# Attention and GELU layers on one core: opening with four-bank exponentials and split numerators, two output tiles in turns, the last one in column halves

## The chip, the core and the metric

The kernel runs on one core of a Trainium2 chip. A core has five engines that run side by side: TensorE (PE, matrix products; its weight loads are listed apart as PEld), VectorE (DVE), ScalarE (ACT), GpSimd (POOL) and SyncE (SP, which here only issues transfers). Each takes its own instructions in the order of the program and waits on semaphores for the others. PE writes its results to PSUM, which has 8 banks of 512 fp32 columns on 128 partitions. The other data lies in SBUF. Transfers are issued by SP or by POOL and run on 16 DMA engines.

The metric is the device time of one execution in microseconds. The kernel before takes 344.38 us (median of three runs, 344.34 to 344.93).

## The reference

```
# q, k, v: (8, 8, 576, 64) fp32; f: (8, 8, 576); w_in: (512, 2048); w_out: (2048, 512)
scores = q @ k^T / 8
cum    = cumsum(log(clip(f, 1e-4, 1)))
scores = where(j > i, -1e9, scores + cum[i] - cum[j])
attn   = softmax(scores) @ v                      # per batch and head
x      = attn, heads side by side                 # (4608, 512)
out    = gelu_tanh(x @ w_in) @ w_out              # (4608, 512) fp32
```

The factor exp(cum[i]) cancels in the softmax. So the kernel takes exponentials of the plain scores and scales the rows of v, and the weights of the denominators, by exp(-cum[j] - 64).

## The kernel before

The 64 pairs of batch and head are worked on in 16 *quads* of four heads. Quads 2b and 2b + 1 belong to batch b.

For each quad there are three **score rounds** (`score_round`). A round computes up to 512 columns of transposed scores for four heads into two PSUM tiles of two banks each. Two `ACTIVATE Exp` instructions (L190), each over one tile (128 x 1024 elements), write them to `pt` as bf16. In the opening the causal mask is added on PE by extra products with `lows` (L186). Later it is POOL that zeroes the entries of `pt` (`mask`, L202).

Three **products** per quad follow (`product`, L218): denominators (weights `w_bf`), and the numerators for the even and the odd half of the head dimension (weights `vw`, which `make_vw` builds out of `v_nat` and `wT` at L140). `reciprocals` turns the denominators into `rb` by a transpose, a reciprocal and a transpose on DVE (L240 to L244). `normalise` multiplies a numerator in PSUM by `rb` into `xT` on DVE (L249).

For each batch `mlp_in` multiplies `xT` by `w_in_sb` in 16 blocks `ft` of 128 hidden features (L263, 8 matmuls of 288 columns each), and ACT applies the GELU (L272) into `gT`. `mlp_out` is a generator: each step is one `ft` of one output tile of 128 tokens (one matmul of 512 columns, or four on 32 rows each). After the 16th step of a tile DVE copies the PSUM tile to SBUF (L300) and SP sends it out (L301). Its PSUM pool has two tiles of one bank. The steps are pulled between the score rounds of coming quads, in numbers written out by hand: for batch 0, 3 and then 14, 8 and 8 in the rounds of quad 2, 5, 6 and 5 in those of quad 3, 4, 4 and 3 in those of quad 4. So the 33rd step is the last of quad 2's third round.

PSUM before: tag `s` two tiles of two banks, `po` one tile of two banks, and the last two banks are `x` (one tile) in the opening and `m` (two tiles of one bank) afterwards.

The **opening** (`startup`) loads f, q, k and v, forms `cum` and `wT`, transposes k and q of quads 0 and 1, and runs six score rounds and six products. Warm-up matmuls on a blank tile keep PE busy at the start and between the rounds (L319, 11, then 6, then 4 after each of the first four rounds). Its loads on POOL's queue, in order: k and q of quads 0 and 1, v (heads 4 to 7 of batch 0), w_in in four transfers of 512 KB, k and q of quad 2, w_out in four transfers, k and q of quad 3, and v of batch 1 (heads 0 to 3, five transfers). SP issues v of batch 1 (heads 4 to 7) once q of quad 3 has landed. POOL's issues wait so that no more than eight of its transfers are under way. The order of instructions on each engine is that of the code (`manual_schedule`).

In `step(i, j, ...)`, which runs the three rounds of quad i with the products of quad j, quads 2 and 3 have `make_vw` on DVE in the third round, ahead of that round's pull of output steps. Later quads have it on POOL in the first.

Of the kernel before, what the change touches and what calls it, by code (L numbers as in the profile page):

```python
# [8 lines left out]
FP32 = mybir.dt.float32  # L9
BF16 = mybir.dt.bfloat16  # L10
AF = mybir.ActivationFunctionType
# [5 lines left out]
def kernel(  # L17
# [10 lines left out]
    nc = tc.nc  # L28
# [30 lines left out]
    psS = ctx.enter_context(tc.tile_pool(name="psS", bufs=2, space=bass.MemoryType.PSUM))  # L59
    psO = ctx.enter_context(tc.tile_pool(name="psO", bufs=1, space=bass.MemoryType.PSUM))  # L60

    def many(n, shape, dtype, name):
        return [singles.tile(shape, dtype, name=f"{name}{i}") for i in range(n)]
# [14 lines left out]
    w_in_sb = many(2, [128, N_DT, D_FF // 2], BF16, "w_in_sb")  # L78
# [10 lines left out]
    pools = {"s": psS, "po": psO}  # L89


    def after(ins, other):

# [20 lines left out]
    w_out_hbm = moe_w_out.rearrange("(u p y) n -> p u y n", p=128, y=2)  # L114

    def load_w_in(c):
        n = slice(D_FF // 2 * c, D_FF // 2 * (c + 1))
        for u in range(QPB):
            nc.gpsimd.dma_start(out=w_in_sb[c][:, 2 * u:2 * u + 2, :], in_=w_in_hbm[u, :, :, n])  # L119

    def load_w_out(c):
        n = N_FT // 8
# [21 lines left out]
    def bank_pair(tag, name):  # L144
        return pools[tag].tile([128, 2, 512], FP32, name=name, tag=tag)
# [9 lines left out]
    def score_round(i, r, tags=("s", "s"), masked=False):  # L155
        off, parts = rounds[r]
        n = sum(x[2] for x in parts)
        tiles = [bank_pair(x, "ps_s") for x in tags]
        kk, qq, p = kT[i % 2], qT[i % 2], pt[i % 2]
        def block(c, m0, m, k0, q0, nq, c0, fresh):  # L160
            for h in range(4):
                nc.tensor.matmul(  # L162
                    tiles[h // 2][m0:m0 + m, h % 2, c0:c0 + nq],
                    kk[32 * h:32 * h + 32, k0:k0 + m, c],
                    qq[32 * h:32 * h + 32, q0:q0 + nq, c],
                    start=(c == 0 and fresh), stop=(c == 1),
                    skip_group_check=True,
                )
# [12 lines left out]
        if masked:  # L181
            for g in range(2):
                c0 = 0
                for (t, q0, nq) in parts:
                    for x in range(2 if q0 == 128 * t else 0):
                        nc.tensor.matmul(tiles[g][:, x, c0:c0 + 128], ident, lows[t > 0],  # L186
                                         start=False, stop=True, skip_group_check=True)
                    c0 += nq
        for g in range(2):
            nc.scalar.activation(p[:, 2 * g:2 * g + 2, off:off + n],  # L190
                                 tiles[g][:, :, 0:n], AF.Exp, scale=scale)
# [59 lines left out]
    def denominators(i):  # L251
        reciprocals(i, product(i, den_groups(i), bank_pair("po", "po")))

    def attn_out(i, y, tag="po"):
        normalise(i, y, product(i, out_groups(i, y), bank_pair(tag, "po")))

    def mlp_mm(b, ft, ph, dts):
        hS = S // 2
        n = 256 * (ft // 2) % (D_FF // 2)
        w = w_in_sb[2 * ft // N_FT][:, :, n + ft % 2:n + 256:2]  # L260
        for dt in dts:
            for j in range(2):
                nc.tensor.matmul(  # L263
                    ph[:, j, 0:hS],
                    w[:, dt],
                    xT[b % 2][:, dt, hS * j:hS * (j + 1)],
                    start=(dt == 0), stop=(dt == N_DT - 1),
                )
# [7 lines left out]
    def mlp_in(b, fts, tag="s"):  # L276
        tiles = [bank_pair(tag, "ps_h") for _ in fts]
        for dts in (range(N_DT - 1), range(N_DT - 1, N_DT)):
            for ft, ph in zip(fts, tiles):
                mlp_mm(b, ft, ph, dts)  # L280
        for ft, ph in zip(fts, tiles):
            gelu(b, ft, ph)


    out_cols = [128]

    def mlp_out(tiles):

        for n in tiles:
            ps = pools["m"].tile([128, D_MODEL], FP32, name="pso", tag="m")  # L290
            c = 128 * (n % 9)
            for ft in range(N_FT):
                w = out_cols[0]
                for m in range(0, 128, w):
                    nc.tensor.matmul(ps[m:m + w, :], gT[:, ft, c + m:c + m + w],  # L295
                                     w_out_sb[:, ft, :], start=(ft == 0),
                                     stop=(ft == N_FT - 1), skip_group_check=True)
                if ft == N_FT - 1:
                    st = ostage_pool.tile([128, D_MODEL], FP32, name="o_st", tag="o")
                    nc.vector.tensor_copy(st, ps)  # L300
# [20 lines left out]
    def startup():  # L321
# [6 lines left out]
        make_lows()  # L328

        nc.vector.memset(blank, 0.0)  # L330
        warm = bank_pair("po", "warm")
        warm_up(warm, 11)
        nc.vector.memset(ones_f32, 1.0)
        nc.vector.memset(shift, -64.0)
# [9 lines left out]
        cum = bank_pair("x", "small")[:, 0, 0:NT * BH]  # L344
# [12 lines left out]
        make_vw(1, nc.vector)  # L357
        load_w_in(0)
        load_w_in(1)
        load_qk(2)  # L360
# [6 lines left out]
        for r, tags in enumerate((("s", "s"), ("x", "s"), ("s", "x"))):  # L367
            score_round(0, r, tags, True)
            warm_up(warm, 4)
        score_round(1, 0, masked=True)  # L370
        warm_up(warm, 4)
        score_round(1, 1, ("x", "s"), True)
        denominators(0)
        score_round(1, 2, ("s", "x"), True)
        attn_out(0, 0)
        attn_out(0, 1, "s")
        pod, po0, po1 = (bank_pair(x, "po") for x in ("s", "po", "x"))
        reciprocals(1, product(1, den_groups(1), pod))
        r0 = product(1, out_groups(1, 0), po0)
        r1 = product(1, out_groups(1, 1), po1)  # L380
        ph0, ph1 = (bank_pair("s", "ps_h") for _ in range(2))
        mlp_mm(0, 0, ph0, (0, 1))
        normalise(1, 0, r0)
        normalise(1, 1, r1)
# [16 lines left out]
    def step(i, j, fill, fills):  # L401
        for r in range(3):
            if i is not None:
                score_round(i, r)
            if j is not None:
                if r == 0:
                    denominators(j)
                else:
                    attn_out(j, r - 1, "s" if i is None and r == 1 else "po")
            if (i, r) in ((2, 0), (3, 1)):  # L410
                transpose_qk(i + 1)
            if i is not None and r > 0:
                mask(i, r - 1)
            if i is not None and r == (2 if i < 4 else 0):
                make_vw(i, nc.vector if i < 4 else nc.gpsimd)
            pull(fill, fills[r], 32)
            if i is not None and r == 2:
                mask(i, 2)
                if i == 2:
                    load_v(2)  # L420
                elif i < 5:
                    load_qk(i + 2)
# [7 lines left out]
                    load_qk(i + 2)  # L430

    with tc.manual_schedule():
        with tc.tile_pool(name="psX", bufs=1, space=bass.MemoryType.PSUM) as pools["x"]:
            startup()
        pools["m"] = ctx.enter_context(
            tc.tile_pool(name="psM", bufs=2, space=bass.MemoryType.PSUM))
        fill = none
        for b in range(B):

# [7 lines left out]
                if b + 2 < B:  # L447
                    load_v(b + 2)
            for ft in range(2, N_FT):
                mlp_in(b, (ft,), "po" if b == 0 and ft == 2 else "s")  # L450
            fill = mlp_out(out_tiles(b))
            if b == 0:
                pull(fill, 3)
# [41 lines left out]
```

## Time and profile before

| | |
|---|---|
| median of 3 runs | 344.38 us (344.34 to 344.93) |
| the profiled execution | 345.22 us |
| its span, first to last instruction | 343.5 us |
| PE busy | 333.7 us (97%) |
| ACT busy | 198.8 us (58%) |
| DVE busy | 125.3 us (36%) |
| POOL busy | 113.7 us (33%) |
| granted PE clock | 1.00 |

A row of a timeline gives the start in us, the busy time, the engine, the line of the kernel, the operation, the tile written and the tiles read, their shapes and how many instructions were merged into the row. In brackets stands the idle time ahead of it and what ended that wait. A row of the groups gives, behind the bar, the busy time and the mean duration in ns of one, and behind the second bar the idle time before them. PE's instructions are pipelined, so the rows of neighbouring products overlap. A row of a window of DMA queues gives the queue, its packets, MB, and the time of its packets as a share of 16 engines (it may pass 100%). A row of issues gives the number of transfers, the KB of each and the median time from issue to landing.

### The profile page before, as it was taken

What the parts mean: (1) busy time and instruction counts of PE and PEld (TensorE: products, weight loads), DVE (VectorE), ACT (ScalarE), POOL (GpSimd) and SP (SyncE); (2) the same over time, 40 slices, a digit from 0 to 9 for tenths busy, and PEclk for the clock granted to TensorE, in tenths of its full rate; (3) what the DMA queues carried; (4) which work ended last, traced back from release to release, by engine and by line L of the source; (5) the groups of instructions that cost most, each with busy time, mean ns of one, the idle gap of its engine ahead of it and who ended that gap; (6) DMA issues with size and microseconds to landing.
All of it is one profiled execution on the core that took longest, in us unless ns stands there. A gap on an engine that the chain in (4) does not pass through costs nothing.

```text
span 343.5 us, 11040 instructions
## 1 busy us (share of the span) xinstructions
PE 333.7 (97%) x5032; PEld 198.1 (58%) x5050; DVE 125.3 (36%) x169; ACT 198.8 (58%) x244; POOL 113.7 (33%) x157
## 2 busy tenths in 40 slices
PE   7989999899999999999999999999999999999995
PEld 2457634477445764467444774457544675557642
DVE  7591167550451513541333503434233402530011
ACT  4866677766655666656746566656745566516400
POOL 6742344844262503524163132624044401200000
PEclk9999999999999999999999999999999999999999
DMA  7899998779110870139111490109111100110021
GB/s 128 177 168 211 211 193 202 149 139 225 44 65 32 171 138 32 63 78 205 28 66 57 106 204 23 48 32 213 27 47 52 62 1 2 35 63 31 2 87 66
DMA packets 45439, 33.37 MB, mean 97 GB/s; under 512 B 34288, under 2 KB 34288, under 8 KB 45392
## 3 DMA queue, kind: packets, MB, share of 16 engines
q0 software_dynamic: 7232, 14.81, 24.3%
q1 hardware_dynamic: 38160, 17.85, 19.6%
q8 instruction: 39, 0.64, 0.8%
q14 instruction: 8, 0.07, 0.1%
HBM read 36.85 MB, written 9.44 MB: 135 GB/s over the span
## 4 chain that ended last, share of the span: by engine, by line
PE 80%; DMA 11%; issue 2%; ACT 2%; POOL 2%; SPq 2%; DVE 1%; POOLq 0%; ACTq 0%
PE ps_h L263 32%; PE pso L295 32%; PE po L218 8%; PE ps_s L162 7%; DMA w_out_sb<-in_moe_w_out_dram 5%; DMA w_in_sb<-in_moe_w_in_dram 3%; DMA q_c<-in_q_dram 2%; ACT pt L190 2%; SPq L105 1%; POOL v_nat L105 1%; DMA v_nat<-in_v_dram 1%; POOL k_c L99 0%; DVE den L240 0%; DVE o_st L300 0%; POOL w_in_sb L119 0%
## 5 line engine op out<-in xcount | busy, mean ns | idle before, releaser
L295 PE MATMUL pso<-w_out_sb,gT 128*32 128x512 bf16 (+1 forms) x1892 | 131.6, 379 | 1.1 <-DMA w_out_sb<-in_moe_w_out_dram 0.4
L263 PE MATMUL ps_h<-xT,w_in_sb 128*128 128x288 bf16 x1024 | 128.3, 286 | 0.7 <-DMA w_in_sb<-in_moe_w_in_dram 0.7
L190 ACT ACTIVATE pt<-ps_s 128x1024 bf16<-128x1024 f32 x96 | 93.0, 1021 | 50.0 <-PE ps_s L162 47.6
L272 ACT ACTIVATE gT<-ps_h 128x576 bf16<-128x576 f32 x128 | 82.5, 651 | 64.7 <-PE ps_h L263 64.6
L263 PEld LDWEIGHTS <-w_in_sb 128*128 128x128 bf16 x1024 | 99.5, 98 | 30.4 <-issue 3.2
L295 PEld LDWEIGHTS <-gT 128*32 128x32 bf16 (+1 forms) x1908 | 59.0, 97 | 54.0 <-issue 1.5
L202 POOL TENSOR_SCALAR_AFFINE_SELECT pt<-pt 128x512 bf16<-128x512 bf16 (+1 forms) x70 | 45.3, 656 | 125.4 <-ACT pt L190 124.4
L300 DVE COPY o_st<-pso 128x512 f32<-128x512 f32 x36 | 24.6, 684 | 63.0 <-PE pso L295 62.8
L240 DVE STREAM_TRANSPOSE den<-po 128x576 f32<-128x576 f32 x16 | 12.5, 782 | 80.5 <-PE po L218 80.5
L249 DVE TENSOR_TENSOR xT<-po,rb 128x576 bf16<-128x576 f32 x32 | 24.1, 757 | 44.9 <-PE po L218 44.5
L162 PE MATMUL ps_s<-qT,kT 32*64 32x64 bf16 (+6 forms) x896 | 36.1, 292 | 1.4 <-DVE qT L130 0.5
L140 POOL TENSOR_TENSOR vw<-v_nat,wT 128x1280 bf16<-128x1280 f32 (+1 forms) x24 | 34.8, 1473 | 1.6 <-PE po L218 1.5
L162 PEld LDWEIGHTS <-kT 32*128 32x128 bf16 (+1 forms) x896 | 15.1, 97 | 26.9 <-issue 23.3
L218 PE MATMUL po<-pt,vw 128*32 128x64 bf16 (+4 forms) x768 | 27.3, 279 | 0.3 <-DVE den L240 0.3
L130 DVE STREAM_TRANSPOSE kT<-k_c 128x576 f32<-128x576 f32 x16 | 19.9, 1246 | 19.5 <-DMA k_c<-in_k_dram 19.5
L218 PEld LDWEIGHTS <-vw 128*32 128x32 bf16 x768 | 13.2, 97 | 14.0 <-issue 7.0
L130 DVE STREAM_TRANSPOSE qT<-q_c 128x576 f32<-128x576 f32 x16 | 19.9, 1243 | 0.8 <-DMA q_c<-in_q_dram 0.6
L99 POOL DMA_DIRECT2D k_c<-in_k_dram x16 | 9.1, 568 | 31.6 <-DVE kT L130 26.6
L218 PE MATMUL po<-pt,w_bf 128*32 128x512 bf16 (+5 forms) x384 | 14.3, 279 | 0.9 <-POOL pt L202 0.9
L244 DVE STREAM_TRANSPOSE rb<-rec 128x576 f32<-128x576 f32 x16 | 12.5, 779 | 0.5
L190 ACT ACT_TABLE_LOAD x7 | 9.0, 1283 | 5.9 <-PE ps_s L162 5.9
L99 POOL DMA_DIRECT2D q_c<-in_q_dram x16 | 8.7, 544 | 9.7 <-DVE qT L130 5.3
(38 smaller groups left out, 72.9 us busy)
## 6 DMA issues: line engine op xcount, KB each, us to landing
out_dram<-o_st SPq DMA_DIRECT2D x36, 256.0 KB, 2.0
v_nat<-in_v_dram SPq DMA_DIRECT2D x24, 256.0 KB, 7.1
k_c<-in_k_dram POOLq DMA_DIRECT2D x16, 288.0 KB, 6.3
q_c<-in_q_dram POOLq DMA_DIRECT2D x16, 288.0 KB, 7.1
w_in_sb<-in_moe_w_in_dram POOLq DMA_DIRECT2D x4, 512.0 KB, 10.9
w_out_sb<-in_moe_w_out_dram POOLq DMA_DIRECT2D x4, 512.0 KB, 18.5
v_nat<-in_v_dram SPq DMA_DIRECT2D x14, 128.0 KB, 5.8
v_nat<-in_v_dram POOLq DMA_DIRECT2D x8, 128.0 KB, 7.0
```

Source lines behind the costliest of these rows:

```text
L99: return [nc.gpsimd.dma_start(out=dst[i % 2].rearrange("p a d -> p (a d)"), in_=src[b, h0:h0 + 4].rearrange("h (p a) d -> (h p) (a d)", p=32))
L130: nc.vector.transpose(out=dst[i % 2].rearrange("p s c -> p (s c)").bitcast(FP32) .rearrange("p (t a) -> p a t", a=S // 32), in_=src[i % 2] ...
L140: eng.tensor_mul(vw[i % 2][:p, slot:slot + n], v_nat[(i // QPB) % 2][:p, 0:n, h0:h0 + 4, :], wT[:p, i, 0:n, :].unsqueeze(3).to_broadcast([ ...
L162: nc.tensor.matmul(tiles[h // 2][m0:m0 + m, h % 2, c0:c0 + nq], kk[32 * h:32 * h + 32, k0:k0 + m, c], qq[32 * h:32 * h + 32, q0:q0 + nq, c ...
L190: nc.scalar.activation(p[:, 2 * g:2 * g + 2, off:off + n], tiles[g][:, :, 0:n], AF.Exp, scale=scale)
L202: nc.gpsimd.affine_select(out=p[p0:p1, :, o:o + 128], in_=p[p0:p1, :, o:o + 128], compare_op=ALU.is_ge, fill=0.0, base=0, pattern=[[0, 4]] ...
L218: nc.tensor.matmul(po[r0:r0 + w.shape[-1], o:o + nq], w, p[:, h, col:col + nq], start=(n < 2), stop=(n in (0, len(product_parts) - 1)), sk ...
L249: nc.vector.tensor_mul(xT[i // QPB % 2][:, 2 * (i % QPB) + y, :], po, rbs[i])
L263: nc.tensor.matmul(ph[:, j, 0:hS], w[:, dt], xT[b % 2][:, dt, hS * j:hS * (j + 1)], start=(dt == 0), stop=(dt == N_DT - 1),)
L272: nc.scalar.activation(gT[:, ft, o:o + S].rearrange("p (j n) -> p j n", j=2), ph[:, :, 0:hS], AF.Gelu_apprx_tanh)
L295: nc.tensor.matmul(ps[m:m + w, :], gT[:, ft, c + m:c + m + w], w_out_sb[:, ft, :], start=(ft == 0), stop=(ft == N_FT - 1), skip_group_chec ...
L300: nc.vector.tensor_copy(st, ps)
```

## The change

1. **PSUM and exponentials in the opening.** A pool `q` of two tiles of four banks takes all eight banks while `startup` runs. A score round fills one tile, and one `ACTIVATE Exp` of 128 x 2048 elements reads all four banks. The warm-up matmuls between the rounds are gone; the 11 and the 6 ahead of them stay. All six rounds come first, and the products follow in `first_products`, in pools `s`, `po` and `x` that are opened when `q` is closed.
2. **Numerators of quad 0.** ACT copies each of the two from PSUM to SBUF (`num`), and POOL multiplies them by `rb`. Before, DVE multiplied straight out of PSUM. The loads of w_out, of k and q of quad 3 and of v of batch 1 are issued after these two POOL products.
3. **w_in in three tiles**, of 512, 512 and 1024 columns: six transfers in place of four.
4. **Output tiles 0 and 1** take turns: 12 steps of tile 0, 12 of tile 1, the last 4 of tile 0, the last 4 of tile 1. Tile 2 follows as before, with step 33.
5. **`make_vw` of quad 3** goes from DVE in the third round to POOL in the second.
6. **The last output tile** is computed in two column halves: 16 matmuls of 256 columns, a copy and a transfer for each half.
7. Block `ft` = 2 of batch 0 uses a tile of tag `s` in place of `po`.

```diff
+        if whole:
+            four = pools["q"].tile([128, 4, 512], FP32, name="ps_s", tag="q")
+            tiles = [four[:, 0:2, :], four[:, 2:4, :]]
...
+            nc.scalar.activation(p[:, :, off:off + n], four[:, :, 0:n], AF.Exp, scale=scale)
+            return
...
     def mlp_out(tiles):
+        half, open_ps = D_MODEL // 2, {}
+        most, whole = range(N_FT - 4), [(n, range(N_FT), 0, D_MODEL) for n in tiles]
+        if tiles[0] == 0:
+            whole[0:2] = [(n, fts, 0, D_MODEL) for fts in (most, range(N_FT - 4, N_FT))
+                          for n in tiles[0:2]]
+        if tiles[-1] == B * S // 128 - 1:
+            whole[-1:] = [(tiles[-1], range(N_FT), c0, c0 + half) for c0 in (0, half)]
+        for n, fts, c0, c1 in whole:
+            if fts[0] == 0:
+                open_ps[n] = pools["m"].tile([128, D_MODEL], FP32, name="pso", tag="m")
...
                 if ft == N_FT - 1:
                     st = ostage_pool.tile([128, D_MODEL], FP32, name="o_st", tag="o")
-                    nc.vector.tensor_copy(st, ps)
-                    nc.sync.dma_start(out=out[128 * n:128 * n + 128, :], in_=st)
+                    nc.vector.tensor_copy(st[:, c0:c1], ps[:, c0:c1])
+                    nc.sync.dma_start(out=out[128 * n:128 * n + 128, c0:c1], in_=st[:, c0:c1])
...
+        for i in range(2):
+            for r in range(3):
+                score_round(i, r, True)
+
+    def first_products():
+        denominators(0, "s")
+        nums = []
+
+        def copy_out(y):
+            num = den_pool.tile([128, S], FP32, name="num", tag="num")
+            nc.scalar.copy(num, product(0, out_groups(0, y), bank_pair("s", "po")))
+            nums.append(num)
+
+        copy_out(0)
+        reciprocals(1, product(1, den_groups(1), bank_pair("po", "po")))
+        copy_out(1)
+        for y in range(2):
+            nc.gpsimd.tensor_mul(xT[0][:, y, :], nums[y], rbs[0])
         for c in range(4):
             load_w_out(c)
...
+        r0 = product(1, out_groups(1, 0), bank_pair("x", "po"))
+        r1 = product(1, out_groups(1, 1), bank_pair("s", "po"))
+        ph0, ph1 = bank_pair("s", "ps_h"), bank_pair("po", "ps_h")
...
-            if i is not None and r == (2 if i < 4 else 0):
-                make_vw(i, nc.vector if i < 4 else nc.gpsimd)
+            if i is not None and r == {2: 2, 3: 1}.get(i, 0):
+                make_vw(i, nc.vector if i == 2 else nc.gpsimd)
...
+        with psum("psQ", 2) as pools["q"]:
             startup()
+        pools["s"] = ctx.enter_context(psum("psS", 2))
+        pools["po"] = ctx.enter_context(psum("psO", 1))
+        with psum("psX", 1) as pools["x"]:
+            first_products()
+        pools["m"] = ctx.enter_context(psum("psM", 2))
```

More of the change, by code (lines that the diff above doesn't have):

```diff
@@ L77 @@
     gT = singles.tile([128, N_FT, 2 * S], BF16, name="gT")
-    w_in_sb = many(2, [128, N_DT, D_FF // 2], BF16, "w_in_sb")
+    w_in_sb = [singles.tile([128, N_DT, D_FF // n], BF16, name=f"w_in_sb{n}{x}")
+               for n, x in ((4, 0), (4, 1), (2, 0))]
     w_out_sb = singles.tile([128, N_FT, D_MODEL], BF16, name="w_out_sb")
@@ L153, in make_lows, with score_round @@
                     base=0, pattern=pattern, channel_multiplier=-1)
-    def score_round(i, r, tags=("s", "s"), masked=False):
+    def score_round(i, r, whole=False):
         off, parts = rounds[r]
         n = sum(x[2] for x in parts)
-        tiles = [bank_pair(x, "ps_s") for x in tags]
+        if whole:
+            four = pools["q"].tile([128, 4, 512], FP32, name="ps_s", tag="q")
+            tiles = [four[:, 0:2, :], four[:, 2:4, :]]
+        else:
+            tiles = [bank_pair("s", "ps_s") for _ in range(2)]
         kk, qq, p = kT[i % 2], qT[i % 2], pt[i % 2]
@@ L274, in gelu, with mlp_in @@
             ph[:, :, 0:hS], AF.Gelu_apprx_tanh)
-    def mlp_in(b, fts, tag="s"):
-        tiles = [bank_pair(tag, "ps_h") for _ in fts]
+    def mlp_in(b, fts):
+        tiles = [bank_pair("s", "ps_h") for _ in fts]
         for dts in (range(N_DT - 1), range(N_DT - 1, N_DT)):
@@ L287, in mlp_out @@
     def mlp_out(tiles):
[L289 to L292, printed above, removed]
+        half, open_ps = D_MODEL // 2, {}
[8 more added lines that the diff above has]
+                open_ps[n] = pools["m"].tile([128, D_MODEL], FP32, name="pso", tag="m")
+            ps, c = open_ps[n], 128 * (n % 9)
+            for ft in fts:
                 w = out_cols[0]
                 for m in range(0, 128, w):
-                    nc.tensor.matmul(ps[m:m + w, :], gT[:, ft, c + m:c + m + w],
-                                     w_out_sb[:, ft, :], start=(ft == 0),
+                    nc.tensor.matmul(ps[m:m + w, c0:c1], gT[:, ft, c + m:c + m + w],
+                                     w_out_sb[:, ft, c0:c1], start=(ft == 0),
                                      stop=(ft == N_FT - 1), skip_group_check=True)
@@ L330, in startup @@
         nc.vector.memset(blank, 0.0)
[L331 removed]
+        warm = pools["q"].tile([128, 4, 512], FP32, name="warm", tag="q")
         warm_up(warm, 11)
```

45 lines of the change are left out of this document (15 added, 30 removed).

## The prediction

> **What bounds the kernel now.** I read the busy times by stage first, then the timeline of each engine where a stage leaves TensorE (PE) idle.
>
> ```profile
> 25.50:40.30 14.80, 14.79 (x120) 11.75 (x121) 3.08 (x3) 9.67 (x15) 4.73 (x7) 1.00 1.12 211
> ...
> 44.36:72.00 27.64, 26.52 (x515) 13.24 (x516) 18.68 (x24) 19.50 (x21) 16.64 (x23) 1.00 0.78 157
> 72.00:343.50 271.50, 266.30 (x4005) 160.35 (x4017) 84.67 (x114) 149.71 (x187) 76.27 (x95) 1.00 0.32 77
> ```
>
> The columns are stretch, length, then busy time of PE, weight loads, VectorE (DVE), ScalarE (ACT), GpSimd (POOL), granted clock, DMA share and GB/s. From 25.5 us on PE is nearly full (271.5 us of the last stretch hold 266.3 of work). In the first of these stretches the DMA engines are full too (share 1.12). So a gain must be made before 72 us, where PE has little idle time, or behind the last matmul. The waits that end last there:
>
> ```profile
> 18.59 1.42 POOL L123 DMA_DIRECT2D w_out_sb<-in_moe_w_out_dram  x2
> ...
> 32.34 0.54 POOL L99 DMA_DIRECT2D q_c<-in_q_dram  x1 [3.30 <-DMA w_in_sb<-in_moe_w_in_dram]
> ...
> 42.09 0.63 POOL L105 DMA_DIRECT2D v_nat<-in_v_dram  x1 [1.71 <-DMA w_out_sb<-in_moe_w_out_dram]
> ```
> ```profile
> v_nat<-in_v_dram POOLq DMA_DIRECT2D x1, 64.0 KB, 6.7
> ```
> ```profile
> 44.36 1.26 PE L295 MATMUL pso<-w_out_sb,gT 128*32 128x512 bf16 x20 [0.42 <-DMA w_out_sb<-in_moe_w_out_dram]
> ```
>
> The last w_in load has landed by 32.3 us, the last w_out load at about 44.3, and the fifth v load of batch 1 (heads 0 to 3) at 42.09 + 6.7 = 48.8 us. These loads follow each other in one full queue. The change leaves their order and their bytes alone, so it cannot bring them forward.
>
> **The opening (exponentials, numerators of quad 0).**
>
> ```profile
> 9.59 11.99 ACT L190 ACTIVATE pt<-ps_s 128x1024 bf16<-128x1024 f32 x12 [1.94 <-PE ps_s L186]
> ...
> 19.33 0.77 DVE L240 STREAM_TRANSPOSE den<-po 128x576 f32<-128x576 f32 x1
> ...
> 20.15 1.55 PE L218 MATMUL po<-pt,vw 128*32 128x64 bf16 x48 [0.32 <-DVE den L240]
> ...
> 20.43 0.78 DVE L244 STREAM_TRANSPOSE rb<-rec 128x576 f32<-128x576 f32 x1
> ```
> ```profile
> 25.51 14.98 PE L263 MATMUL ps_h<-xT,w_in_sb 128*128 128x288 bf16 x120 [0.68 <-DMA w_in_sb<-in_moe_w_in_dram]
> ```
> ```profile
> L190 ACT ACTIVATE pt<-ps_s 128x1024 bf16<-128x1024 f32 x96 | 93.0, 1021 | 50.0 <-PE ps_s L162 47.6
> L272 ACT ACTIVATE gT<-ps_h 128x576 bf16<-128x576 f32 x128 | 82.5, 651 | 64.7 <-PE ps_h L263 64.6
> ```
> ```profile
> L140 POOL TENSOR_TENSOR vw<-v_nat,wT 128x1280 bf16<-128x1280 f32 x12 | 28.0, 2336 | 1.6 <-PE po L218 1.5
> ```
>
> Twelve exponentials now fill ACT from 9.59 to 21.58. The two ACT rows give (1021 - 651) / 448 = 0.83 ns an element, so one instruction of 2048 takes 1021 + 1024 x 0.83 = 1.87 us; in a train, with the 50 ns that neighbours overlap (96 x 1021 = 98.0 against 93.0 busy), 1.82. Six take 10.9 us. The first waits for both masks, 0.1 us more: ACT ends near 20.6, 0.9 us earlier. (From nothing saved at all, 21.6, to the bare slope, 19.9.)
>
> What follows: denominators of quad 0 need the banks of the fifth round, free at 9.7 + 5 x 1.82 = 18.8, and PE gives 0.78 a product (48 matmuls in 1.55). DVE takes 1.88 from denominators to rb (19.33 to 21.21), so rb0 is there at 18.85 + 0.8 + 1.9 = 21.55. ACT copies num0 at 20.65 to 21.3 (0.65, the 576-wide row). PE goes on: denominators 1 to 21.5, second numerator to 22.3, its copy to 22.95, r0 and r1 to 23.85. POOL multiplies 576 elements in 1.05 us by the row of 1280 (2336 ns): num0 21.6 to 22.65, num1 23.0 to 24.05. Then 14 more matmuls of 0.1225 us: the block ft = 2 starts at about 25.9, where before it was 25.51 + 8 x 0.1225 = 26.5. PE leads by about 0.5 us. Its bounds are a lag of 1.3 (a copy that loads a table, or a handover of banks that waits for all six exponentials) and a lead of 1.5. w_in's last quarter is needed at ft = 8, at 25.51 + 60 x 0.1225 = 32.9 before and 32.4 now, about when it lands (32.3). POOL's two products stand ahead of the w_out issues, which move from 18.6 to about 24; they cost nothing, because the queue still holds w_in until 32.3. If that cover were gone they would cost 24 - 18.6, 5.4 us.
>
> The smaller w_in pieces make 512 more packets of half the size. A bound is the cost of whole short packets:
>
> ```profile
> q1 hardware_dynamic: 1802, 0.46, 120.0%
> ```
>
> In that stretch of 2 us a packet of 256 bytes took 16 x 2 x 1.2 / 1802 = 21 ns, so at most 512 x 21 / 16 = 0.7 us, at least nothing; much of the 21 ns is data, so I take 0.2 us, on all loads behind.
>
> **The two first output tiles in turns.** The last w_out chunk is needed at the 25th step, not the 13th: the wait of 0.42 us goes, at most 0.42 gained. But tile 0 is now complete at step 28 instead of 16. Step 33 opens tile 2 in tile 0's bank and waits for the copy of tile 0. That copy is now issued behind make_vw(2) on DVE, which is in order:
>
> ```profile
> 47.15 1.26 DVE L130 STREAM_TRANSPOSE qT<-q_c 128x576 f32<-128x576 f32 x1
> 48.26 0.68 DVE L300 COPY o_st<-pso 128x512 f32<-128x512 f32 x1
> 48.92 1.92 DVE L140 TENSOR_TENSOR vw<-v_nat,wT 128x1280 bf16<-128x1280 f32 x2
> 50.76 0.67 DVE L300 COPY o_st<-pso 128x512 f32<-128x512 f32 x1
> ```
> ```profile
> 48.83 1.91 PE L295 MATMUL pso<-w_out_sb,gT 128*32 128x512 bf16 x32
> 50.67 0.91 PE L162 MATMUL ps_s<-qT,kT 32*64 32x512 bf16 x24
> ```
>
> make_vw(2) needs the v load: 48.8 + 0.2 = 49.0, ends 50.9, the copy ends 51.55. Step 33 lay at 50.67 - 0.23 = 50.44 and now starts at 51.6: the scores of quad 3 come at 51.83 instead of 50.67, 1.15 us later, and this whatever the opening gained; a lag of the opening up to about 1.2 disappears in it as well. Bounds: 0.55 (make_vw(2) right behind qT at 48.4) to 1.65 (the full 0.7 of the packets).
>
> **make_vw(3) from DVE to POOL.**
>
> ```profile
> 58.68 2.24 DVE L140 TENSOR_TENSOR vw<-v_nat,wT 128x1280 bf16<-128x1280 f32 x2
> ```
> ```profile
> L202 POOL TENSOR_SCALAR_AFFINE_SELECT pt<-pt x15: 627/637/1574, 47.1 to 69.5; 128x512 bf16<-128x512 bf16 x9, 64x512 bf16<-64x512 bf16 x6
> ```
> ```profile
> 57.07 1.94 ACT L190 ACTIVATE pt<-ps_s 128x1024 bf16<-128x1024 f32 x2 [0.73 <-PE ps_s L162]
> 59.87 1.94 ACT L190 ACTIVATE pt<-ps_s 128x1024 bf16<-128x1024 f32 x2 [0.86 <-PE ps_s L162]
> ```
> ```profile
> 51.50 0.96 PE L218 MATMUL po<-pt,w_bf 128*32 128x64 bf16 x24
> 52.29 1.25 PE L295 MATMUL pso<-w_out_sb,gT 128*32 128x512 bf16 x20
> ...
> 59.65 0.65 PE L218 MATMUL po<-pt,w_bf 128*32 128x64 bf16 x16
> ...
> 61.47 0.25 PE L218 MATMUL po<-pt,w_bf 128*1 128x192 bf16 x4 [0.46 <-POOL pt L202]
> 61.55 1.03 PE L295 MATMUL pso<-w_out_sb,gT 128*32 128x512 bf16 x16
> ...
> 65.24 0.63 PE L162 MATMUL ps_s<-qT,kT 32*128 32x320 bf16 x14 [0.18 <-ACT pt L190]
> ```
>
> One mask beside DVE's make_vw(3) took 1574 ns where the median is 637, and PE waited for it: denominators 3 took 61.55 - 59.65 = 1.90 us, those of quad 2 52.29 - 51.50 = 0.79. Without that product on DVE the masks follow the exponentials (59.01 + 1.15 = 60.16) at 0.64 each and end at 61.5; denominators 3 start at 60.8 and end at 61.6 instead of 61.55. The lag of 1.15 is down to 0.05. Then the exponentials of quad 4, round 0 end 1.15 later (62.96), the next scores need their bank: 62.96 + 0.04 + 0.68 of matmuls, the following pair of exponentials ends at 65.62, and the scores at 65.24 come at 65.66. Net +0.42 us (-0.15 to +0.9 by the bounds). Behind this nothing waits, so it stays.
>
> **The last tile in halves.**
>
> ```profile
> 339.69 0.69 DVE L300 COPY o_st<-pso 128x512 f32<-128x512 f32 x1 [2.76 <-PE pso L295]
> ```
> ```profile
> GB/s 0 0 0 0 0 0 0 0 0 0 0 0 0 0 0 0 0 0 0 18 364 364 419 382 364 346 73 0 0 0 0 0 0 0 0 0 0 0 0 0
> ```
>
> Columns are slices of 4.5 / 40 = 0.11 us. The last copy (0.69) becomes one of 256: between 0.35 (half) and 0.6, taken 0.41. The transfer (six full slices, 0.7) halves: -0.35. So -0.63 in all, at most. PE runs the same columns. No row shows a matmul into a bank that a copy is reading. If the second half waits for the first copy, it adds 0.41 and a restart of 0.2 to 0.3: +0.05 net. Without the wait -0.6. I take the wait, the first copy and the second half being of one tile.
>
> [...]
>
> **Sum.** +0.42 + 0.05 = +0.47 against the profiled execution of 345.22 us (span 343.5 and 1.7 around it), or, its extra 0.84 taken off, 344.38 + 0.47 = 344.85 us. I count 0.2% (0.69 us: 343.69 and 345.07) as the least that can be told from no change.
>
> **Rivals.**
> 1. *Tail overlapped*: 344.85 - 0.65 = 344.2. For it: the halves touch different columns.
> 2. *No wait at step 33* (copy of tile 0 ahead of make_vw(2)). Then the lead of 0.5, the 0.42 of w_out and the 0.87 of the masks' waits (0.41 + 0.46) all stay: 344.38 - 1.79 = 342.6. Against it: DVE kept the order of the code in the four rows above.
> 3. *POOL late with make_vw(3)* (slower):
>
> ```profile
> 47.08 2.08 POOL L202 TENSOR_SCALAR_AFFINE_SELECT pt<-pt 64x512 bf16<-64x512 bf16 x3
> ...
> 53.70 1.36 POOL L202 TENSOR_SCALAR_AFFINE_SELECT pt<-pt 64x512 bf16<-64x512 bf16 x2 [1.55 <-ACT pt L190]
> ```
>
> Behind the masks of round 0 (55.06 + 1.15 = 56.2) it holds POOL for 2.34 and, at the same 1.83 ns an element, 0.47 us, so mask (3,1) is done near 59.7; denominators 3 come to it at about 61.0. Beside DVE's transposes for quad 4 it could be held as masks were beside a product, 2 x 1.25 us. From about 0.5 us of delay on it moves the masks of round 2, due at 60.16; at 2.5 us it costs 2.0: 346.85. Against it: the three masks at 47.08 took 0.69 each beside the transpose at 47.15.
> 4. *Clock lost in the opening* (slower), since 16 warm-up matmuls between the rounds go:
>
> ```profile
> 1.26 4.88 PE L319 MATMUL warm<-blank 128*128 128x512 bf16 x11 [1.26 <-DVE blank L330]
> ...
> 6.76 1.47 PE L319 MATMUL warm<-blank 128*128 128x512 bf16 x6
> ```
>
> Matmuls took 0.44 us each at first, 0.22 later. At half rate for another 5 us the opening loses 2.5; less 0.5 of lead and 1.2 that step 33 takes in, +0.8: 345.7. Against it: the gaps left between rounds are under 0.8 us. [...] The granted clock here is 1.00 throughout, and no run here shows it.
>
> **Chances.** Forecast 0.48 (own range 344.2 to 345.3), tail overlapped 0.14, no wait 0.18, POOL late 0.10, clock 0.10. Faster: the 0.18, a fifth of the overlapped tail and a tenth of the forecast, 0.25. Slower: 0.20 and a seventh of the forecast, 0.27. Same: 0.48. The range 342.7 to 345.9 leaves out half of rival 2 and nearly all of rival 3.
>
> **What would show it.** Six exponentials of 1.87 us ending near 20.6; ft = 2 at 25.9; PE idle about 1.4 us before a pso matmul at 51.6, released by DVE's copy, which starts at 50.9 behind make_vw(2); no PE wait for a mask near 61 us, masks at 0.64; at 44.3 no wait for w_out; in the last 8 us a PE gap of about 0.5 us between the halves. I am wrong if the scores of quad 3 start before 51.2 us, if the v load of batch 1 lands much before 48.8, or if PE's score matmuls near 12 us pace at half rate.

## The result and the profile after

| | before | after |
|---|---|---|
| median of 22 runs each | 344.85 us (344.15 to 347.06) | 345.78 us (345.14 to 346.67) |
| ratio | | 1.0028 (95%: 1.0018 to 1.0039) |
| the profiled execution | 345.22 us | 345.89 us |
| its span | 343.5 us | 344.1 us |

The change makes the kernel slower by 0.28% (about 0.95 us). The forecast was +0.47 us (0.14%, which counts as no change by its bound of 0.2%). The sign and the range were right, but the sum is half of the loss, which lies just beyond that bound and is made of different terms. By the prediction's own count the outcome is "slower", to which it gave 0.27.

The waits of PE in the changed kernel (us in total, times, longest):

```profile
PE po L226 <- ACT pt L195: 2.3, 1, 2.3
PE ps_s L168 <- ACT pt L195: 2.0, 4, 1.1
...
PE ps_h L272 <- POOL xT L398: 0.5, 1, 0.5
PE ps_s L168 <- ACT pt L198: 0.4, 2, 0.3
```

The two waits for masks (0.9 us) and the one for w_out (0.4) are gone. In their place PE waits 2.3 us for an exponential ahead of its first product, and no wait for DVE's copy shows at step 33. The timeline from there:

```profile
10.15 10.77 ACT L195 ACTIVATE pt<-ps_s 128x2048 bf16<-128x2048 f32 x6 [2.17 <-PE ps_s L192]
...
20.97 1.52 PE L226 MATMUL po<-pt,w_bf 128*32 128x64 bf16 x24 [2.35 <-ACT pt L195]
...
22.26 1.57 PE L226 MATMUL po<-pt,vw 128*32 128x64 bf16 x24
...
23.93 0.65 ACT L391 COPY num<-po 128x576 f32<-128x576 f32 x1 [3.01 <-PE po L226]
...
24.67 2.88 POOL L398 TENSOR_TENSOR xT<-num,rb 128x576 bf16<-128x576 f32 x2 [4.88 <-ACT num L391]
...
27.60 2.61 PE L272 MATMUL ps_h<-xT,w_in_sb 128*128 128x288 bf16 x20 [0.51 <-POOL xT L398]
```

The six exponentials take 10.77 us, as forecast (10.9). But the first product starts at 20.97, when the sixth has ended, and not at 19.2, when the fifth has. Each of the first two products then takes 1.3 us (20.97 to 22.26 to 23.59), not 0.8. Block ft = 2 starts at 27.60 + 14 x 0.1225 = 29.3 us. Before the change it started at 26.5, and the forecast was 25.9. The stage windows show why the products were slow (columns as in the prediction; the third from the end is the granted clock):

```profile
12.00:13.50 1.50, 1.19 (x24) 0.90 (x24) 1.14 (x3) 1.50 (x2) 1.50 (x3) 1.00 0.57 143
13.50:15.30 1.80, 1.45 (x28) 0.76 (x27) 1.14 (x2) 1.80 (x2) 1.80 (x4) 0.59 0.64 187
15.30:17.20 1.90, 1.75 (x22) 0.75 (x21) 0.12 (x1) 1.90 (x2) 1.90 (x3) 0.50 0.81 120
17.20:19.00 1.80, 1.19 (x24) 0.92 (x25) 1.70 (x2) 1.80 (x2) 1.80 (x4) 0.99 0.98 121
19.00:20.90 1.90, 0.00 (x0) 0.00 (x0) 0.00 (x0) 1.90 (x2) 0.79 (x2) 0.94 1.17 170
20.90:22.20 1.30, 1.23 (x24) 0.63 (x27) 0.00 (x0) 0.02 (x1) 0.00 (x0) 0.50 1.23 199
22.20:23.50 1.30, 1.30 (x32) 0.77 (x28) 0.85 (x2) 0.00 (x0) 0.00 (x0) 0.50 1.19 189
```

The clock is halved twice in this execution: among the score rounds, and again after the idle 2.35 us. The first time costs nothing, since the rounds still fit under the exponentials of 1.8 us. The second time the products pay.

How the lag shrinks on its way (one row of PE's timeline before, then the changed kernel's):

```profile
40.33 0.81 PE L295 MATMUL pso<-w_out_sb,gT 128*128 128x512 bf16 x2
```

```profile
43.03 0.81 PE L313 MATMUL pso<-w_out_sb,gT 128*128 128x512 bf16 x2
...
52.83 0.73 PE L168 MATMUL ps_s<-qT,kT 32*64 32x512 bf16 x24
...
61.51 0.96 PE L226 MATMUL po<-pt,w_bf 128*32 128x64 bf16 x24
62.30 1.03 PE L313 MATMUL pso<-w_out_sb,gT 128*32 128x512 bf16 x16
...
66.42 0.63 PE L168 MATMUL ps_s<-qT,kT 32*128 32x320 bf16 x14 [0.16 <-ACT pt L198]
```

Against the rows of before, PE is late by 43.03 - 40.33 = 2.70 at the first output step, 2.16 at the scores of quad 3, 1.86 at the denominators of quad 3, 62.30 - 61.55 = 0.75 behind them, and 66.42 - 65.24 = 1.18 two rounds on. It then stays 1.18 late: the copy of tile 34, the last that is whole in both kernels, starts at 337.42, and before it started at 336.24. DVE at the end, before and then after:

```profile
336.24 0.69 DVE L300 COPY o_st<-pso 128x512 f32<-128x512 f32 x1 [2.76 <-PE pso L295]
```

```profile
337.42 0.69 DVE L318 COPY o_st<-pso 128x512 f32<-128x512 f32 x1 [2.76 <-PE pso L313]
339.17 0.42 DVE L318 COPY o_st<-pso 128x256 f32<-128x256 f32 x1 [1.05 <-PE pso L313]
340.92 0.42 DVE L318 COPY o_st<-pso 128x256 f32<-128x256 f32 x1 [1.32 <-PE pso L313]
```

The half copies lie 1.75 us apart, which is just 16 matmuls of 0.109: the second half does not wait for the first copy. The code gives the reason. In the diff above, `mlp_out` takes a new tile of tag `m` whenever a run of steps begins with `ft` = 0, and both halves begin with it. So each half has a PSUM tile of its own, and tag `m` has two tiles of one bank each: the second half is written to another bank than the one that DVE is copying. From the copy of the last whole tile to the end of the span it is 6.68 us, where it was 7.26: 0.58 us gained. So 1.18 - 0.58 = +0.60 us, the difference of the spans.

### The profile page after: what moved, and what is told of

It reads as the page before. It is cut to its first block, busy times and chain, and to the rows that moved or that the text cites. A ratio compares the mean times of both kernels' runs of the same rounds, so it can differ in the third digit from the quotient of the medians.

```text
span 344.1 us, 11033 instructions
## 1 busy us (share of the span) xinstructions
PE 332.0 (96%) x5034; PEld 199.6 (58%) x5050; DVE 122.5 (36%) x166; ACT 199.2 (58%) x240; POOL 119.7 (35%) x163
## 3 DMA queue, kind: packets, MB, share of 16 engines
HBM read 36.85 MB, written 9.44 MB: 135 GB/s over the span
## 4 chain that ended last, share of the span: by engine, by line
PE 88%; ACT 6%; issue 2%; DMA 2%; POOL 1%; DVE 0%; ACTq 0%; POOLq 0%
PE ps_h L272 37%; PE pso L313 33%; PE po L226 9%; PE ps_s L168 8%; ACT pt L195 3%; ACT pt L198 2%; DMA q_c<-in_q_dram 2%; POOL xT L398 1%; DVE qT L132 0%; ACT num L391 0%; POOL k_c L100 0%; DVE o_st L318 0%; PE ps_s L192 0%; ACT L198 0%; ACTq L198 0%
## 5 line engine op out<-in xcount | busy, mean ns | idle before, releaser
L313 PE MATMUL pso<-w_out_sb,gT 128*32 128x512 bf16 (+2 forms) x1908 | 131.6, 377 | 0.7
L198 ACT ACTIVATE pt<-ps_s 128x1024 bf16<-128x1024 f32 x84 | 81.4, 1021 | 46.9 <-PE ps_s L168 46.9
L313 PEld LDWEIGHTS <-gT 128*32 128x32 bf16 (+1 forms) x1924 | 60.6, 97 | 52.3 <-issue 1.0
L210 POOL TENSOR_SCALAR_AFFINE_SELECT pt<-pt 128x512 bf16<-128x512 bf16 (+1 forms) x70 | 44.1, 638 | 128.2 <-ACT pt L198 127.2
L318 DVE COPY o_st<-pso 128x512 f32<-128x512 f32 (+1 forms) x37 | 24.8, 671 | 64.3 <-PE pso L313 64.2
L257 DVE TENSOR_TENSOR xT<-po,rb 128x576 bf16<-128x576 f32 x30 | 22.6, 756 | 45.1 <-PE po L226 44.9
L142 POOL TENSOR_TENSOR vw<-v_nat,wT 128x1280 bf16<-128x1280 f32 (+1 forms) x26 | 37.8, 1472 | 0.2
L226 PE MATMUL po<-pt,vw 128*32 128x64 bf16 (+4 forms) x768 | 28.0, 283 | 0.0
L100 POOL DMA_DIRECT2D k_c<-in_k_dram x16 | 9.2, 572 | 29.4 <-DVE kT L132 26.5
L226 PEld LDWEIGHTS <-w_bf 128*1 128x1 bf16 (+1 forms) x384 | 6.5, 90 | 9.7 <-issue 5.6
L195 ACT ACTIVATE pt<-ps_s 128x2048 bf16<-128x2048 f32 x6 | 10.8, 1878 | 2.2 <-PE ps_s L192 2.2
```

Source lines behind the costliest of these rows:

```text
L142: eng.tensor_mul(vw[i % 2][:p, slot:slot + n], v_nat[(i // QPB) % 2][:p, 0:n, h0:h0 + 4, :], wT[:p, i, 0:n, :].unsqueeze(3).to_broadcast([ ...
L195: nc.scalar.activation(p[:, :, off:off + n], four[:, :, 0:n], AF.Exp, scale=scale)
L198: nc.scalar.activation(p[:, 2 * g:2 * g + 2, off:off + n], tiles[g][:, :, 0:n], AF.Exp, scale=scale)
L210: nc.gpsimd.affine_select(out=p[p0:p1, :, o:o + 128], in_=p[p0:p1, :, o:o + 128], compare_op=ALU.is_ge, fill=0.0, base=0, pattern=[[0, 4]] ...
L226: nc.tensor.matmul(po[r0:r0 + w.shape[-1], o:o + nq], w, p[:, h, col:col + nq], start=(n < 2), stop=(n in (0, len(product_parts) - 1)), sk ...
L313: nc.tensor.matmul(ps[m:m + w, c0:c1], gT[:, ft, c + m:c + m + w], w_out_sb[:, ft, c0:c1], start=(ft == 0), stop=(ft == N_FT - 1), skip_gr ...
```

## The experiments

All ratios are against the kernel before, timed on the same chip. "The changed kernel" has 1.0028.

**Halves alone.** The kernel before, with:

```diff
+        if tiles[-1] == B * S // 128 - 1:
+            whole[-1:] = [(tiles[-1], range(N_FT), c0, c0 + half) for c0 in (0, half)]
...
```

> The kernel before with one edit: the last output tile in two column halves. Theory A (the halves overlap, as the two copies 1.75 us apart in the changed kernel suggest): the way from the start of the copy of the last whole tile to the end of the span shrinks from 7.26 us to about 6.7, the time falls by 0.55 us (0.16%). Theory B (the second half waits for the first copy): the two half copies lie about 2.4 us apart and the time stays within 0.1 us.

Ratio 0.9979 (0.9969 to 0.9988): 0.7 us gained, with the half copies at 337.37 and 339.12, 1.75 us apart, as in the changed kernel. Theory A holds: the halves overlap. That they lie in two banks, as above, is true of this kernel too.

**Turns alone.** The kernel before, with:

```diff
+        if tiles[0] == 0:
+            whole[0:2] = [(n, fts, 0, D_MODEL) for fts in (most, range(N_FT - 4, N_FT))
+                          for n in tiles[0:2]]
...
```

> The kernel before with one edit: output tiles 0 and 1 in turns (12, 12, 4 and 4 steps). Theory A (step 33 waits for the copy of tile 0, which stands behind make_vw(2) on DVE; the changed kernel hid this behind a late opening): PE idles over 1 us near 50.5 us, released by DVE's copy, which starts at the end of make_vw(2); the scores of quad 3 start at 51.7 instead of 50.67 and the time rises by 0.8 to 1.2 us. Theory B (no such wait): the 0.42 us wait for w_out at 44.3 goes and the time falls by 0.2 to 0.4 us.

Ratio 1.0018 (1.0008 to 1.0029), 0.6 us lost. PE, then DVE, of this run:

```profile
50.84 0.40 PE L301 MATMUL pso<-w_out_sb,gT 128*32 128x512 bf16 x4 [0.61 <-DVE o_st L306]
51.17 0.67 PE L162 MATMUL ps_s<-qT,kT 32*64 32x512 bf16 x24
```
```profile
47.93 2.26 DVE L140 TENSOR_TENSOR vw<-v_nat,wT 128x1280 bf16<-128x1280 f32 x2 [0.69 <-DMA v_nat<-in_v_dram]
50.12 1.27 DVE L306 COPY o_st<-pso 128x512 f32<-128x512 f32 x2
```

The wait at step 33 is there, behind make_vw(2), but it is 0.61 us and not over 1, and the loss is below the 0.8 to 1.2 us of theory A: the v load had landed by 47.9 us, 1 us earlier than forecast from one execution. The next run shows how much such landings vary.

**w_in in three tiles alone.** The kernel before, with six transfers for four:

```diff
-    w_in_sb = many(2, [128, N_DT, D_FF // 2], BF16, "w_in_sb")
+    w_in_sb = [singles.tile([128, N_DT, D_FF // n], BF16, name=f"w_in_sb{n}{x}")
+               for n, x in ((4, 0), (4, 1), (2, 0))]
...
```

> The kernel before with one edit: w_in in three tiles. Theory A (the landing times differ between executions of one kernel by 1.5 us, and the pieces are no cause of it): any wait of PE for w_in before the first blocks is gone, DVE's xT takes its place (about 0.6 us), kT of quad 3 starts between 43.7 and 46.0 us as in the other profiles, and the time stays within 0.3 us. Theory B (short pieces bring the loads forward by 1.5 us): kT of quad 3 starts at 42.5 us or earlier.

Ratio 1.0002 (0.9991 to 1.0013), kT of quad 3 at 45.04 us. Over the profiles of the runs that keep the opening of before, that transpose starts between 43.7 and 46.0 us. The profile of before was the latest of them, and its wait of 0.42 us for w_out shows in none of the others.

**make_vw(3) on POOL alone.** The kernel before, with:

```diff
-            if i is not None and r == (2 if i < 4 else 0):
-                make_vw(i, nc.vector if i < 4 else nc.gpsimd)
+            if i is not None and r == {2: 2, 3: 1}.get(i, 0):
+                make_vw(i, nc.vector if i == 2 else nc.gpsimd)
```

> The kernel before with one edit: make_vw of quad 3 on POOL in the second round. Theory A (the masks were held by DVE's product): both masks of quad 3, round 2 take 0.64 us, PE's two waits for them (0.41 and 0.46 us) go, and after the wait for the exponentials of quad 4 about 0.6 us is left: the time falls by 0.5 to 0.7 us. Theory B (POOL is late with make_vw(3)): PE waits longer for the masks and the time rises by up to 2 us.

Ratio 0.9984 (0.9974 to 0.9994): 0.55 us gained. Denominators 3 take 0.78 us (1.90 before), the masks 0.61 each, and PE waits 0.42 us in all for the exponentials of quad 4, where it waited 0.18 before. The rows show the first of these waits:

```profile
59.30 0.95 PE L218 MATMUL po<-pt,w_bf 128*32 128x64 bf16 x24
60.08 1.03 PE L295 MATMUL pso<-w_out_sb,gT 128*32 128x512 bf16 x16
...
61.50 0.63 PE L162 MATMUL ps_s<-qT,kT 32*128 32x64 bf16 x14 [0.26 <-ACT pt L190]
```

**The opening alone.** The changed kernel without these three edits (turns, halves, POOL's make_vw(3)).

> The changed kernel with the output tiles one after the other and whole, and make_vw of quad 3 on DVE, as before: the opening and the three w_in tiles alone. Theory A (the opening is 2.7 us later and nothing behind it takes that in; the halves and POOL's make_vw give back 1.2 us in the changed kernel): the time is 1.9 to 2.8 us above the kernel before (0.55 to 0.8%). Theory B (most of the late opening is taken in by later waits): it is under 1.2 us above.

Ratio 1.0053 (1.0036 to 1.0070): 1.8 us lost, just under the range of theory A; theory B's 1.2 us is below the interval. The parts fit within their intervals: 0.53% less 0.21% and 0.16% leaves 0.16%, and the whole measured 0.28% (0.18 to 0.39).

**The first four products in the opening's pool.** The changed kernel, with:

```diff
+        return [pools["q"].tile([128, 4, 512], FP32, name="po", tag="q") for _ in range(2)]
...
+        reciprocals(0, product(0, den_groups(0), t0[:, 0:2, :]))
...
+        copy_out(0, t0[:, 2:4, :])
+        reciprocals(1, product(1, den_groups(1), t1[:, 0:2, :]))
+        copy_out(1, t1[:, 2:4, :])
```

> The changed kernel with one edit: the first four products write into two further four-bank tiles of the opening's pool, not into a new pool. Theory A (the wait of 2.35 us before the first product comes from the handover of the pool, which waits for the sixth exponential and not for the fifth): the first product starts near 19.1 us, the block ft = 2 starts near 27 us instead of 29.3, and, since step 33 then waits for DVE's copy (ready at 50.9), the scores of quad 3 come at 51.2 instead of 52.83; the time falls by 1.2 to 1.6 us against the changed kernel, so 0.3 to 0.8 us below the kernel before. Theory B (the slow clock is the cause, the handover only its company): the first product still starts near 21 us and the time stays as in the changed kernel, 0.9 us above the kernel before.

The time does not fall: ratio 1.0047 (1.0028 to 1.0067). The full timeline says where theory A was right and what ate it:

```profile
18.92 0.86 PE L226 MATMUL po<-pt,w_bf 128*32 128x64 bf16 x24 [0.58 <-ACT pt L195]
...
20.67 0.87 PE L226 MATMUL po<-pt,vw 128*32 128x64 bf16 x24 [0.88 <-DVE den L248]
...
23.10 0.87 PE L226 MATMUL po<-pt,vw 128*32 128x64 bf16 x24 [0.88 <-DVE den L248]
...
24.70 1.55 PE L226 MATMUL po<-pt,vw 128*32 128x64 bf16 x48 [0.74 <-ACT num L392]
...
28.15 1.28 ACT L281 ACT_TABLE_LOAD   x1 [3.50 <-PE ps_h L272]
```

The first product does start with the end of the fifth exponential, and products take 0.9 us. But two products that share a tile wait for each other's readers (0.88 us twice), the next pool waits for the copy of num (0.74), and the table load for the GELU now comes only behind the first block (PE then waits 0.85 for ACT). Since this edit makes new waits, the next one moves a single product:

**One product in the opening's pool.**

```diff
+        four = pools["q"].tile([128, 4, 512], FP32, name="po", tag="q")
+        reciprocals(0, product(0, den_groups(0), four[:, 0:2, :]))
 
     def first_products():
-        denominators(0, "s")
```

> The changed kernel with one edit: only the denominators of quad 0 go to a further tile of the opening's pool, all other products to the new pools. Theory A (the handover and the idle gap behind it make the opening late): the first product starts near 19 us, the other products follow from 20.7 us at 0.8 us each, ft = 2 starts near 27 us instead of 29.3; then step 33 waits for DVE's copy by 0.5 to 1.5 us, and the time is 0.3 to 0.8 us below the kernel before. Theory B (POOL's and ACT's chain or the clock sets the opening anyway): ft = 2 stays above 28.4 us and the time is at or above that of the kernel before.

Ratio 0.9992 (0.9981 to 1.0004): 1.2 us below the changed kernel, level with the kernel before, and a little above the time that theory A named (0.3 to 0.8 us below). The twelve runs are of two kinds. Six had a mean granted clock of 1.00 and took 344.0 to 344.4 us, with a median 0.6 us below the kernel before (344.71 beside them), as theory A said. Six had 0.99 and took 344.0 to 345.6. The profiled run is one of the first six. Its timeline, and further on PE's:

```profile
18.45 0.86 PE L226 MATMUL po<-pt,w_bf 128*32 128x64 bf16 x24 [0.58 <-ACT pt L195]
...
20.22 0.87 PE L226 MATMUL po<-pt,vw 128*32 128x64 bf16 x24 [0.91 <-ACT pt L195]
...
24.75 5.43 PE L272 MATMUL ps_h<-xT,w_in_sb 128*128 128x288 bf16 x43 [0.58 <-POOL xT L399]
```
```profile
51.00 0.40 PE L313 MATMUL pso<-w_out_sb,gT 128*32 128x512 bf16 x4 [1.28 <-DVE o_st L318]
```

ft = 2 starts at 24.75 + 1.72 = 26.5 us, as early as before the change, and 2.8 us earlier than in the changed kernel. Of these, 0.7 us are due to the execution: the exponentials began at 9.44 us, not at 10.15. Step 33 takes 1.28 us of that back: this is the wait that the prediction named, seen once the opening is on time.

**The idle gap filled.** The changed kernel, with eight blank matmuls between the last round and the first product:

```diff
+        warm_up(pools["q"].tile([128, 4, 512], FP32, name="warm", tag="q"), 8)
```

> The changed kernel with eight warm-up matmuls more, into a further tile of the opening's pool, in the gap between the last score round and the first product. Theory A (the idle gap of 2.35 us takes the clock back a second time, and the first products pay for it): the clock is near 1.00 from 20.9 to 24.5 us, a product takes 0.8 us there and not 1.3, num of the first half is copied near 22.6 instead of 23.93, ft = 2 starts 1.0 to 1.3 us earlier, and the time falls by about 1.0 us against the changed kernel, to within 0.4 us of the kernel before. Theory B (the chain over ACT and POOL sets the end of the opening, whatever PE's clock): ft = 2 moves by less than 0.3 us and the time stays 0.9 us above the kernel before.

Ratio 1.0013 (1.0001 to 1.0024): about 0.5 us of the 1.0 expected, and the interval overlaps that of the changed kernel. The clock was 1.00 from 9 us on, in the rounds too. num was copied at 22.45 and products took 0.7 us. ft = 2 came at 26.65 + 1.72 = 28.4, which is 0.9 us earlier, 0.4 of it because the exponentials began at 9.75 here. POOL is now the last to be ready:

```profile
26.65 3.59 PE L272 MATMUL ps_h<-xT,w_in_sb 128*128 128x288 bf16 x28 [0.96 <-POOL xT L399]
```

Step 33 took back 0.54 us. As the clock did not fall in the rounds of this execution either, which the edit does not touch, this profile does not show alone that the filling kept it up. Two other readings support it. With the first four products in the old pool, the clock fell to 0.53 among the rounds, as in the changed kernel, but was back at 1.00 from 17.2 us on and stayed there through gaps of 0.9 us at most. And the mean granted clock of the timed runs was 0.985 to 0.995 in all 22 of the changed kernel, but 0.999 or 1.00 in 8 of the 11 with the gap filled.

**No warm-ups in the old opening.** The kernel before without `warm_up(warm, 4)` after its first four rounds.

> The kernel before without the 16 warm-up matmuls between its score rounds. Theory A (without them PE works about two thirds of each round and the clock is taken back, as in the changed kernel at 13.5 us): the granted clock falls to 0.5 somewhere between 12 and 20 us; the exponentials still set the pace, so the loss comes from the products behind them and the time rises by 0.3 to 1.2 us. Theory B (gaps under a microsecond leave the clock alone and only the gap of 2.35 us in the changed kernel costs it): the clock stays at 1.00 and the time within 0.1 us.

Ratio 1.0046 (1.0029 to 1.0063), 1.6 us lost, somewhat over the range of theory A. The time follows the clock from run to run: four of the twelve runs had a mean granted clock of 0.995 and took 345.3 to 345.7 us, four had 0.99 and took 346.1 to 346.9, four had 0.983 to 0.985 and took 347.2 to 347.6. The profiled run had 0.99. Its clock by stage:

```profile
13.50:15.30 1.80, 1.25 (x26) 0.70 (x24) 1.67 (x2) 1.67 (x3) 1.80 (x3) 1.00 0.61 171
15.30:17.20 1.90, 1.31 (x28) 0.59 (x15) 0.15 (x1) 1.64 (x3) 1.90 (x4) 0.57 0.69 146
17.20:19.00 1.80, 1.66 (x26) 0.73 (x29) 1.07 (x1) 1.26 (x3) 1.80 (x4) 0.50 1.03 147
19.00:20.90 1.90, 1.90 (x36) 0.71 (x32) 1.23 (x3) 1.67 (x2) 1.63 (x3) 0.50 0.96 114
```

From 8 us on no idle stretch of PE was longer than 0.94 us, yet the clock was at or near 0.5 for some 6 us. In this opening the rounds wait for PE at half rate (ACT idles up to 1.24 us), so it costs more.

**Numerators on DVE.** The kernel with the gap filled, with DVE multiplying straight out of PSUM, and the reciprocals of quad 1 behind both numerators:

```diff
-            nc.scalar.copy(num, product(0, out_groups(0, y), bank_pair("s", "po")))
+            nums.append(product(0, out_groups(0, y), bank_pair("s", "po")))
+            normalise(0, y, nums[y])
...
-            nc.gpsimd.tensor_mul(xT[0][:, y, :], nums[y], rbs[0])
```

> The changed kernel with the gap filled as in the run before, and with the numerators of quad 0 multiplied by DVE straight out of PSUM, without ACT's copies and POOL's products. Theory A (DVE, with 0.75 us for each and the denominators of quad 1 queued behind them, is then the bound: rb0 at 23.7, two products to 25.2, rb1 at 27.1, two products to 28.5): ft = 2 starts near 28.9, 0.5 us later than the 28.4 with ACT and POOL, and the time is the same or up to 0.4 us more than with the gap filled alone. Theory B (ACT's copies and POOL's products of 1.4 us are themselves the delay): ft = 2 starts before 27.9 us and the time falls.

Ratio 1.0084 (1.0061 to 1.0106), 2.5 us above the gap filled alone. ft = 2 was due at 27.82 + 0.98 = 28.8, as theory A said, but the time is 2 us over its range:

```profile
27.82 2.30 PE L272 MATMUL ps_h<-xT,w_in_sb 128*128 128x288 bf16 x16 [1.32 <-DVE xT L257]
28.97 1.28 ACT L281 ACT_TABLE_LOAD   x1 [8.60 <-PE ps_h L272]
```

The table load now starts at 28.97, with the first GELU, not at 24.41 behind the copies; PE waits 0.9 us for ACT. It is not that the copies are missing: with the first four products in the old pool both copies were there, and the load came as late (28.15). What decides its place no run here settles. Only a part of the 2.5 us lies in this: the spans of the two profiles, both at a clock of 1.00, differ by 1.2 us (344.9 and 343.7). The rest goes with the clock of the timed runs. The two at 1.00 took 346.6 us, the four at 0.985 to 0.994 took 347.5 to 349.0; why these lost the clock is open.

**Two and three of the edits together.** The kernel before with halves and POOL's make_vw(3); then with w_in in three tiles as well.

> The kernel before with two of the edits: the halves of the last tile and make_vw of quad 3 on POOL. Theory A (the two gains lie at different places and add): 1.1 to 1.3 us below the kernel before, ratio near 0.9965. Theory B (the second gain is taken back by a later wait that the halves do not touch): the ratio is that of the halves alone, 0.998.

> The kernel before with the halves of the last tile, make_vw of quad 3 on POOL and w_in in three tiles. Theory A (the third edit only removes a wait for w_in that DVE's xT mostly covers): 1.1 to 1.5 us below the kernel before, ratio 0.9956 to 0.9968. Theory B (the longer queue of packets costs what it gains): the ratio is above 0.997.

Ratios 0.9965 (0.9953 to 0.9977) and 0.9963 (0.9950 to 0.9977), medians 343.57 and 343.49 us. The two gains add, and w_in in three tiles adds nothing that can be told. Both lie about 1.2 us below the kernel before and 2.2 us below the changed kernel.

## Why the prediction was right, and where it failed

- **Exponentials**: right. 1.878 us each in place of 1.87 forecast, 10.77 us for six. They started 0.45 us later than assumed, because DVE's first transposes of k and q came later in that execution (6.41 and 7.81 us, before 6.11 and 7.37), the first of them behind a wait of 0.15 us for the load of k.
- **Denominators of quad 0 "need the banks of the fifth round, free at 9.7 + 5 x 1.82 = 18.8"**: this step failed. The first product goes to a pool that is opened when the other is closed, and it waited for the sixth exponential, 1.8 us more. With a tile of the old pool it starts at 18.45 and 18.92, 0.58 us behind the last score round in both runs. Whether the new pool waits for the whole old one, or its first tile lies on the banks of the sixth round, no run tells apart. The handover stood among the bounds as a lag of 1.3 us, without the idle gap that follows from it.
- **Clock**: held to be a rival at 0.10, and with the wrong place and price. Its sign did show, though later than 12 us: the 24 score matmuls at 13.85 us took 1.08 us, those at 9.12 only 0.67. This first fall cost nothing in the profiled execution, where ACT stayed busy through the rounds. The loss came from the gap of the handover (two products at 1.3 us). Handover, clock and the late start of 0.45 us made a lag of 2.8 us at ft = 2, where a lead of 0.5 was forecast.
- **POOL's products**: sized 1.05 us from make_vw's row, measured 1.42.
- **Packets of w_in**: 0.2 us forecast on all loads behind; nothing measured. The loads move by up to 2.3 us between the profiled executions (kT of quad 3 starts between 43.7 and 46.0 us). The sum took the landing times of one execution as fixed.
- **Step 33**: the mechanism was right (0.61, 0.54 and 1.28 us in three runs), the size not: +1.15 us forecast, of which 0.5 (51.17 - 50.67) is seen in the turns alone. In the changed kernel it did not show: the opening was so late that the copy was done in time, and the lag at the scores of quad 3 was 2.16.
- **make_vw(3)**: right. Forecast 1.10 us off the lag at the denominators of quad 3, measured 1.86 - 0.75 = 1.11. The later wait for exponentials returned 0.37 by the forecast and 0.43 by the trace. Alone, 0.55 us gained. POOL was not late (rival 3).
- **Tail**: this step failed. The wait between the halves was taken as likely (+0.05 us), "the first copy and the second half being of one tile". They are not of one tile: the code gives each half its own, in another bank, and there is no wait (-0.58). So no run shows that wait, nor the restart of 0.2 to 0.3 us reckoned with it: where PE did wait for a copy (step 33 with one product moved), it went on at 51.00 us, 0.05 behind the end of that copy (50.27 and, by the mean of before, 0.68). Rival 1, given 0.14, is what happened, but not for the reason given there, that the halves touch different columns: each half has its own bank, so no run here puts that reason to the test.
- **Sum**: opening and step 33 instead of +1.15 gave +2.16, the tail instead of +0.05 gave -0.58. Another 0.30 of the lag (2.16 to 1.86) went between the scores and the denominators of quad 3; its cause is not shown. The errors are of opposite sign, and it is luck that the result (+0.60 in the spans, +0.95 in the medians) fell near the forecast.

## What to carry to other kernels

When one PSUM pool replaces another, look for the last reader of the old pool: the first user of the new one may wait for it, as it did here for the sixth exponential (PE idle for 2.35 us). Before pricing a wait on a PSUM tile, look up in the code which tile each user gets. Warm-up work between dependent rounds may be what holds the clock, so time its removal alone: here the granted clock was 1.00 with it and at or near 0.5 for some 6 us without it, and 1.6 us were lost. A landing time from one execution is a sample (here the spread was 2.3 us), so a stall that hangs on it should be given a spread of its own, and edits of one change are worth timing alone: two of these gain 0.35% together, and the opening loses 0.53%.

## What was not expected of the hardware

The granted clock fell to 0.5 without a long idle stretch. In the rounds of the changed kernel the longest before the first fall was 1.07 us, with PE busy about 1.2 us of each 1.8. Rounds of the same matmuls did not always lose it: in the profiled executions they kept 1.00 with the gap filled (there too behind an idle stretch of 1.07 us) and with one product moved, and in the opening alone the clock stayed at 0.5 from 13.5 to 23.5 us. What sets the fall off, and when, no run here shows.

A product of 576 elements on POOL took 1.42 us (2.5 ns an element), where make_vw with its broadcast operand takes 2.34 us for 1280 (1.8 ns).
